# Two KV heads in one set of partitions: even partitions hold one head, odd partitions the other

## The chip, the cores and the metric

The kernel runs on one core of a Trainium2 chip. The metric is the device time of one execution in microseconds (us), the median of several runs. Engines are named as in the profile: PE is TensorE (PEld its weight loads), DVE VectorE, ACT ScalarE, POOL GpSimd, SP SyncE, whose queue issues nearly all DMAs here.

## The reference

One token of a decoder layer, batch 1, float32. The layer norm of x feeds attention over a cached window and a gated MLP, and both are added to x:

```python
xn = layernorm(x)                                    # x: 1 x 1 x 1024
q = (xn @ wq).reshape(32 heads, 128)                 # wq: 1024 x 4096
k, v = k_cache[:, :, -4096:, :], v_cache[:, :, -4096:, :]   # 4 KV heads, 8 query heads to each
p = softmax(q @ k.T * 128 ** -0.5)                   # 32 x 4096
a = (p @ v).reshape(4096) @ wo                       # wo: 4096 x 1024
h = gelu(xn @ w_gate) * (xn @ w_up)                  # 1024 x 3584 each, tanh form
out = x + a + h @ w_down                             # w_down: 3584 x 1024
```

The weights and the two windows of the cache come to 94.4 MB, each byte of which is used once. The window of one KV head is 4096 keys of 128 numbers, 2 MB.

## The kernel before

All weights and cache rows pass through one tile, `ring`, of 128 partitions with 32768 floats each. `PLAN` (L39) lists 17 loads: a key such as ("k", 0), the column of the ring where it begins, and the older load whose place it takes. `used(key)` (L121) issues the loads that wait for `key`, and the main loop (L441) goes through the plan in the same order and consumes each load. So the order of all DMAs is written by hand: wq in two loads of 8.4 MB, then k and v of heads 0 and 1, half of w_gate, k and v of heads 2 and 3, the rest of w_gate, w_up, wo, w_down. All go through SP's queue, in that order. A DMA that overwrites a piece of the ring is held on SP until the engines that read this piece are done, and what stands behind it on SP waits too.

Rows of a matrix are split between PE and DVE in `project` (L227): rows r = 0 and 2 go to PE (`blocks`), rows 1 and 3 are scaled and added into `part` by DVE (L210, L212), and `projected` adds `part` at the end.

A window of keys is read by `window` (L76): partition p takes keys 32p to 32p + 31, 16 KB in one piece. ("k", 0) is two DMAs, head 0 to columns 0 to 4095 of the ring and head 1 to columns 4096 to 8191; ("v", 0) goes to the next 8192 columns likewise, and ("k", 1), ("v", 1) take the same places for heads 2 and 3. For each head `transpose_keys` (L265) makes 32 transposes on PE (`kt_p`), which ACT copies to `kT` (L272), eight copies to a head. `scores` (L275) multiplies them by the head's queries in `qz`; `s_p` then has eight query heads' scores in four quadrants of 32 partitions, 1024 to each. DVE takes the maximum of each partition (L283) and makes `negm`, ACT the exponentials with their sum `l` (L286). `values` (L291) transposes the weights and multiplies them by v into `o_p`. A head's softmax is thus in four parts, one for each quadrant, each with its own maximum; `maxima`, `factors` and `normalizers` bring them to one maximum and one sum, later and away from the loads, and `heads` (L346) weighs `o_p` by them and adds the parts up on PE with `pick`.

Instructions of each engine run in the order in which the code issues them; nothing reorders them.

Of the kernel before, what the change touches and what calls it, by code (L numbers as in the profile page):

```python
# [9 lines left out]
F32 = mybir.dt.float32  # L10
# [5 lines left out]
P = 128  # L16
# [17 lines left out]
SCALE = DH ** -0.5  # L34
GELU_C = math.sqrt(2.0 / math.pi)
# [15 lines left out]
def tile_decode_layer(  # L51
# [24 lines left out]
    def window(cache, g):  # L76
        return cache[0, g, SK - WIN:, :].rearrange("(p j) d -> p j d", p=P)
# [27 lines left out]
    def load(key, at):  # L105

        parts = {("d", 2): 2, ("d", 3): 4}.get(key, 1)
        first = at
        for src in sources(*key):
            rows, n = src.shape[1:]  # L110
            dst = ring[:, at:at + rows * n].rearrange("p (t n) -> p t n", n=n)
            at += rows * n
            step = rows // parts
            for t in range(0, rows, step):
                cuts = 2 if key == ("d", 3) and t == rows - 1 else 1
                for cut in range(cuts):
                    cols = slice(cut * n // cuts, (cut + 1) * n // cuts)
                    nc.sync.dma_start(dst[:, t:t + step, cols], src[:, t:t + step, cols])  # L118
# [26 lines left out]
    qz = consts.tile([P, HKV, 32], F32, name="qz")  # L145
# [97 lines left out]
    def queries():  # L243
# [3 lines left out]
        for b in range(2):  # L247
            for hh in range(4):
# [5 lines left out]
                qz[:, 2 * b:2 * b + 2, 0:8].rearrange("p s (t h) -> p s t h", t=2),  # L254
# [3 lines left out]

    m = work.tile([P, HKV], F32, name="m")
    negm = work.tile([P, HKV], F32, name="negm")  # L260
    l = work.tile([P, HKV], F32, name="l")
# [13 lines left out]
    def scores(g):  # L275
        kT = keys.pop(g)
        s_p = psum.tile([P, 2, NB], F32, name="s_p", tag="s")
        for i in range(8):
            b, c = divmod(i, 4)
            nc.tensor.matmul(  # L280
                s_p[32 * c:32 * c + 32, b, :], qz[:, g, :], kT[:, i, :], start=True, stop=True
            )
        nc.vector.reduce_max(m[:, g:g + 1], s_p, axis=AX.XY)  # L283
        nc.vector.tensor_scalar(negm[:, g:g + 1], m[:, g:g + 1], -SCALE, None, op0=ALU.mult)
        p = work.tile([P, 2, NB], F32, name="p", bufs=2)
        nc.scalar.activation(  # L286
            p, s_p, AF.Exp, bias=negm[:, g:g + 1], scale=SCALE, accum_out=l[:, g:g + 1]
        )
# [26 lines left out]
    top = work.tile([HKV, 4, 32], F32, name="top")  # L315
    weight = work.tile([P, HKV], F32, name="weight")
    sel = same.rearrange("p c h -> p (c h)")

    def maxima():
        mt_p = small("mt_p")  # L320
        nc.tensor.transpose(mt_p[:HKV, :P], m, ident)
        nc.vector.reduce_max(
            top[:, 0, :], mt_p[:HKV, :P].rearrange("g (c h) -> g h c", c=4), axis=AX.X
# [4 lines left out]
    def factors():  # L328
        mm_p = small("mm_p")
        nc.tensor.transpose(mm_p[:, :HKV], top.rearrange("g c h -> g (c h)"), ident[:HKV, :HKV])  # L330
        d = work.tile([P, HKV], F32, name="d")
        nc.vector.tensor_sub(d, m, mm_p[:, :HKV])
        e = work.tile([P, HKV], F32, name="e")
# [12 lines left out]
    def heads():  # L346
        o_sb = work.tile([P, HKV, DH], F32, name="o_sb")
        for g in range(HKV):
            nc.vector.tensor_scalar(
                o_sb[:, g, :], o_p[:, g, :], weight[:, g:g + 1], None, op0=ALU.mult  # L350
# [4 lines left out]
        for odd in range(2):  # L355
            nc.tensor.matmul(
                ot_p, pick[:, odd].rearrange("p o h s -> p (o h s)"),
                o_sb.rearrange("p (a o) d -> p o a d", o=2)[:, odd],
                start=odd == 0, stop=odd == 1,
            )  # L360
# [149 lines left out]
```

## Time and profile before

| | |
|---|---|
| median of 3 runs | 229.1 us (229.05 to 229.22) |
| the profiled execution | 229.1 us; its span on the core is 227.3 us, so 1.8 us lie around it |
| read from HBM | 94.38 MB, 415 GB/s over the span |
| busy share of the span | PE 53%, DVE 43%, ACT 15%, POOL 0% |
| DMA engines | SP's queue q1 takes 97.0% of the 16 engines' span |
| granted TensorE clock | 0.797 |

Busy shares are averages over stages. The row of 40 slices says how busy each engine and the DMA engines are in time; the chain that ended last says what the end of the program hung on, followed back step by step.

### The profile page before, as it was taken

How to read it: one execution, taken by the hardware profiler on the slowest of the kernel's cores; microseconds unless marked ns; L12 is line 12 of the kernel's file. 1: busy time of each engine (PE TensorE's matmuls, PEld its weight loads, DVE VectorE, ACT ScalarE, POOL GpSimd, SP SyncE). 2: the span in 40 equal slices, each digit the busy share in tenths (PEclk: the TensorE clock that was granted, in tenths of full speed). 3: DMA queues.
4: the chain of work that ended last, by engine and by line, in shares of the span. 5: the costliest groups of instructions: out<-in, count | busy, mean ns of one | idle time of the engine just before them, and what ended most of it. 6: DMA issues, size and time to landing. Idle time of an engine off the chain costs nothing.

```text
span 227.3 us, 2496 instructions
## 1 busy us (share of the span) xinstructions
PE 120.4 (53%) x1100; PEld 62.9 (28%) x1100; DVE 97.0 (43%) x105; ACT 33.1 (15%) x57; POOL 0.7 (0%) x6
## 2 busy tenths in 40 slices
PE   0120900687866888595745390255219906452754
PEld 0010200154453746364511010111004903121322
DVE  7030920690202091201149489158219606993600
ACT  2000000054174307453200310000000000000000
POOL 1000000000000000000000000000000000000000
PEclk9999975599679699978879978559956655875879
DMA  9899899799999799999999999999999999999991
GB/s 369 370 461 462 369 484 438 334 438 421 437 484 484 327 424 417 421 510 428 394 407 434 439 469 454 394 493 392 430 461 392 438 412 415 421 456 395 424 385 51
DMA packets 3774, 94.53 MB, mean 416 GB/s; under 512 B 426, under 2 KB 434, under 8 KB 1076
## 3 DMA queue, kind: packets, MB, share of 16 engines
q1 hardware_dynamic: 3752, 94.38, 97.0%
q8 instruction: 8, 0.13, 0.2%
q14 instruction: 2, 0.02, 0.0%
q10 hardware_dynamic: 12, 0.01, 0.0%
HBM read 94.38 MB, written 0.00 MB: 415 GB/s over the span
## 4 chain that ended last, share of the span: by engine, by line
DMA 79%; DVE 14%; PE 5%; issue 0%; SPq 0%; DVEq 0%
DMA ring<-in_B_w_gate 26%; DMA ring<-in_A_wq 18%; DMA ring<-in_A_wo 14%; DVE part L212 13%; DMA ring<-in_B_w_up 11%; DMA ring<-in_B_w_down 10%; PE out_p L421 5%; DVE part L210 1%; SPq L118 0%; DVE y L485 0%; DVEq L212 0%
## 5 line engine op out<-in xcount | busy, mean ns | idle before, releaser
L212 DVE SCALAR_TENSOR_TENSOR part<-ring,xz,part 128x3584 f32<-128x3584 f32 (+1 forms) x9 | 37.2, 4129 | 22.2 <-DMA ring<-in_A_wq 12.4
L271 PE MATMUL kt_p<-ident,ring 128*128 128x128 f32 x128 | 21.5, 327 | 7.0 <-ACT kT L272 6.3
L272 ACT ACTIVATE kT<-kt_p 128x512 f32<-128x512 f32 x32 | 17.8, 595 | 43.9 <-PE kt_p L271 43.9
L222 PE MATMUL acc_q<-ring,xz 128*32 128x512 f32 x64 | 11.1, 858 | 22.2 <-DMA ring<-in_A_wq 22.2
L212 DVE SCALAR_TENSOR_TENSOR out_part<-ring,oz,out_part 128x1024 f32<-128x1024 f32 x15 | 19.3, 1285 | 7.9 <-DMA ring<-in_A_wo 7.4
L421 PE MATMUL out_p<-ring,hz 128*32 128x256 f32 x160 | 14.5, 520 | 13.7 <-DMA ring<-in_B_w_down 13.7
L421 PE MATMUL out_p<-ring,oz 128*32 128x256 f32 x128 | 12.3, 569 | 17.0 <-DMA ring<-in_A_wo 17.0
L271 PEld LDWEIGHTS kt_p<-ident,ring 128*128 128x128 f32 x128 | 16.4, 163 | 15.2 <-ACT kT L272 9.6
L222 PE MATMUL acc_u<-ring,xz 128*32 128x512 f32 x56 | 10.8, 838 | 10.7 <-DMA ring<-in_B_w_up 7.0
L283 DVE TENSOR_REDUCE m<-s_p 128x1 f32<-128x1024 f32 x4 | 4.9, 1224 | 26.7 <-PE s_p L280 26.7
L210 DVE TENSOR_SCALAR part<-ring,xz 128x3584 f32<-128x3584 f32 (+1 forms) x3 | 6.5, 2172 | 14.8 <-DMA ring<-in_A_wq 7.4
L421 PEld LDWEIGHTS out_p<-ring,hz 128*32 128x32 f32 x160 | 6.7, 146 | 21.5 <-DMA ring<-in_B_w_down 12.3
L421 PEld LDWEIGHTS out_p<-ring,oz 128*32 128x32 f32 x128 | 5.5, 162 | 23.9 <-DMA ring<-in_A_wo 18.0
L308 PE MATMUL o_p<-ring,pT 128*32 128x128 f32 x256 | 9.5, 309 | 4.7 <-ACT pT L303 4.7
L212 DVE SCALAR_TENSOR_TENSOR out_part<-ring,hz,out_part 128x1024 f32<-128x1024 f32 x8 | 10.3, 1285 | 3.9 <-DMA ring<-in_B_w_down 3.6
L222 PE MATMUL acc_g<-ring,xz 128*32 128x512 f32 x56 | 8.9, 719 | 4.5 <-DMA ring<-in_B_w_gate 4.5
L222 PEld LDWEIGHTS acc_q<-ring,xz 128*32 128x32 f32 x64 | 2.6, 150 | 29.8 <-issue 15.8
L308 PEld LDWEIGHTS o_p<-ring,pT 128*32 128x32 f32 x256 | 8.0, 123 | 5.8 <-ACT pT L303 5.8
L280 PE MATMUL s_p<-kT,qz 128*32 128x512 f32 x64 | 8.4, 645 | 0.0
L222 PEld LDWEIGHTS acc_u<-ring,xz 128*32 128x32 f32 x56 | 2.1, 138 | 17.6 <-DMA ring<-in_B_w_up 7.7
L178 PE MATMUL xt_p<-ident,x_rows 2*128 2x2 f32 x4 | 0.6, 252 | 10.4 <-DMA x_rows<-in_A_x 10.4
L300 PE MATMUL pt_p<-ident,p 128*128 128x128 f32 x32 | 5.9, 347 | 0.0
(94 smaller groups left out, 76.8 us busy)
## 6 DMA issues: line engine op xcount, KB each, us to landing
ring<-in_B_w_gate SPq DMA_DIRECT2D x2, 7168.0 KB
ring<-in_A_k_cache SPq DMA_DIRECT2D x4, 2048.0 KB
ring<-in_A_v_cache SPq DMA_DIRECT2D x4, 2048.0 KB, 23.3
ring<-in_B_w_down SPq DMA_DIRECT2D x2, 4096.0 KB, 24.3
ring<-in_B_w_up SPq DMA_DIRECT2D x2, 3584.0 KB, 26.3
ring<-in_B_w_up SPq DMA_DIRECT2D x1, 7168.0 KB
ring<-in_B_w_down SPq DMA_DIRECT2D x2, 2048.0 KB, 23.8
ring<-in_B_w_down SPq DMA_DIRECT2D x3, 512.0 KB
```

What stands on the lines that cost most here:

```text
L178: nc.tensor.transpose(xt_p[:, r * NJ:(r + 1) * NJ], x_rows[:, r:NR * P:NR], ident[:NJ, :NJ])
L210: nc.vector.tensor_scalar(total, w, factor, None, op0=ALU.mult)
L212: nc.vector.scalar_tensor_tensor(total, w, factor, total, op0=ALU.mult, op1=ALU.add)
L222: nc.tensor.matmul(acc[kind][32 * c:32 * c + 32, b, :], z, w[:, n * NB:(n + 1) * NB], start=start, stop=stop,)
L271: nc.tensor.transpose(t_p[:, jj * P:(jj + 1) * P], kn[:, j * DH:(j + 1) * DH], ident)
L272: nc.scalar.activation(kT[:, i, :], t_p, AF.Copy)
L280: nc.tensor.matmul(s_p[32 * c:32 * c + 32, b, :], qz[:, g, :], kT[:, i, :], start=True, stop=True)
L283: nc.vector.reduce_max(m[:, g:g + 1], s_p, axis=AX.XY)
L300: nc.tensor.transpose(t_p[:, jj * P:(jj + 1) * P], p[:, b, jj * P:(jj + 1) * P], ident)
L308: nc.tensor.matmul(o_p[32 * c:32 * c + 32, g, :], pT[:, b, jj, 32 * c:32 * c + 32], vn[:, j * DH:(j + 1) * DH], start=(b == 0 and jj == 0) ...
L421: nc.tensor.matmul(out_p[32 * c:32 * c + 32, :], z, w[:, c * CO:(c + 1) * CO], start=start, stop=stop)
```

## The change

`window` now splits the 4096 keys of a head over 64 partitions instead of 128, so each partition takes 64 keys, 32 KB in one piece. The first head of a pair goes to partitions 0, 2, 4, ..., the second to 1, 3, 5, ..., both over the same 8192 columns. There are still eight DMAs of 2 MB for keys and values.

One pass over half of the columns (`transpose_keys`, `scores`, `values` with index g) now has half of the keys of both heads. Its transposes put the two heads' keys in alternate columns, `qz` holds the 16 query heads of a pair, and the scores of a query against the other head's keys are made too and thrown away: `away` is 0 for the head's own keys and -1e30 for the others. It enters the maximum (taken for even and odd columns apart and then joined) and the bias of the exponential, which is made for even and odd columns in two instructions. Each head's softmax is in eight parts, four quadrants times two passes, and `maxima` to `heads` join eight.

```diff
     def window(cache, g):
-        return cache[0, g, SK - WIN:, :].rearrange("(p j) d -> p j d", p=P)
+        return cache[0, g, SK - WIN:, :].rearrange("(p j) d -> p j d", p=P // 2)
...
         first = at
+        if key[0] in "kv":
+            for odd, src in enumerate(sources(*key)):
+                dst = ring[odd:P:2, at:at + RING // 4]
+                nc.sync.dma_start(dst, src.rearrange("p j d -> p (j d)"))
+            loaded[key] = ring[:, at:at + RING // 4]
+            return
...
-    pick = consts.tile([P, 2, 2, REP, 8], F32, name="pick")
-    nc.vector.memset(pick, 0.0)
-    for odd in range(2):
-        nc.vector.tensor_copy(
-            pick[:, odd, odd], same[:, 0, 0:REP].unsqueeze(2).to_broadcast([P, REP, 8])
-        )
+    pick = consts.tile([P, 2 * REP, 8], F32, name="pick")
+    nc.vector.tensor_copy(pick, same[:, 0, 0:2 * REP].unsqueeze(2).to_broadcast([P, 2 * REP, 8]))
...
+    away = consts.tile([P, 2], F32, name="away")
+    nc.vector.reduce_sum(away[:, 1:2], same[:, 0, REP:2 * REP], axis=AX.X)
+    nc.vector.tensor_scalar(away[:, 0:1], away[:, 1:2], -FAR, None, op0=ALU.mult)
+    nc.vector.tensor_scalar(away[:, 1:2], away[:, 1:2], FAR, -FAR, op0=ALU.mult, op1=ALU.add)
...
             nc.tensor.matmul(
-                s_p[32 * c:32 * c + 32, b, :], qz[:, g, :], kT[:, i, :], start=True, stop=True
-            )
-        nc.vector.reduce_max(m[:, g:g + 1], s_p, axis=AX.XY)
-        nc.vector.tensor_scalar(negm[:, g:g + 1], m[:, g:g + 1], -SCALE, None, op0=ALU.mult)
+                s_p[32 * c:32 * c + 32, b, :], qz[:, g // 2, :], kT[:, i, :], start=True, stop=True
+            )
+        s = s_p.rearrange("p b (n odd) -> p odd (b n)", odd=2)
+        m2 = work.tile([P, 2], F32, name="m2")
+        nc.vector.reduce_max(m2, s, axis=AX.X)
+        nc.vector.tensor_add(m2, m2, away)
+        nc.vector.reduce_max(m[:, g:g + 1], m2, axis=AX.X)
+        nc.vector.scalar_tensor_tensor(
+            bias[:, g, :], m[:, g:g + 1].to_broadcast([P, 2]), -SCALE, away, op0=ALU.mult, op1=ALU.add
+        )
         p = work.tile([P, 2, NB], F32, name="p", bufs=2)
-        nc.scalar.activation(
-            p, s_p, AF.Exp, bias=negm[:, g:g + 1], scale=SCALE, accum_out=l[:, g:g + 1]
-        )
+        for odd in range(2):
+            nc.scalar.activation(
+                p.rearrange("p b (n odd) -> p odd (b n)", odd=2)[:, odd], s[:, odd], AF.Exp,
+                bias=bias[:, g, odd:odd + 1], scale=SCALE, accum_out=l[:, g, odd:odd + 1],
+            )
...
         mt_p = small("mt_p")
-        nc.tensor.transpose(mt_p[:HKV, :P], m, ident)
+        for f in range(2):
+            nc.tensor.transpose(mt_p[:2, f * P:(f + 1) * P], m[:, f:HKV:2], ident)
...
         le = work.tile([P, HKV], F32, name="le")
-        nc.vector.tensor_mul(le, l, e)
+        nc.vector.tensor_add(le, l[:, :, 0], l[:, :, 1])
+        nc.vector.tensor_mul(le, le, e.rearrange("p g f -> p (g f)"))
...
-        r = work.tile([P, HKV], F32, name="r")
-        nc.vector.reciprocal(r, ls_p[:, :HKV])
-        nc.vector.tensor_mul(weight, e, r)
+        r = work.tile([P, 2], F32, name="r")
+        nc.vector.reduce_sum(r, ls_p[:, :HKV].rearrange("p (g f) -> p g f", f=2), axis=AX.X)
+        nc.vector.reciprocal(r, r)
+        nc.vector.tensor_mul(weight, e, r.unsqueeze(2).to_broadcast([P, 2, 2]))
...
-        for g in range(HKV):
+        for g in range(2):
             nc.vector.tensor_scalar(
-                o_sb[:, g, :], o_p[:, g, :], weight[:, g:g + 1], None, op0=ALU.mult
+                o_sb[:, g, :], o_p[:, 2 * g, :], weight[:, g, 0:1], None, op0=ALU.mult
+            )
+            nc.vector.scalar_tensor_tensor(
+                o_sb[:, g, :], o_p[:, 2 * g + 1, :], weight[:, g, 1:2], o_sb[:, g, :],
+                op0=ALU.mult, op1=ALU.add,
             )
...
-        for odd in range(2):
-            nc.tensor.matmul(
-                ot_p, pick[:, odd].rearrange("p o h s -> p (o h s)"),
-                o_sb.rearrange("p (a o) d -> p o a d", o=2)[:, odd],
-                start=odd == 0, stop=odd == 1,
-            )
+        nc.tensor.matmul(ot_p, pick.rearrange("p h s -> p (h s)"), o_sb, start=True, stop=True)
```

SP's queue, from the first keys to the second half of w_gate, before the change. Each row is a DMA with its destination's partitions and floats and the semaphores that it is held for: DMAHW are landings of earlier DMAs, PE and DVE are counts of work done there.

```order
L118 DMA ring<-in_A_k_cache 128x4096 [waits DMAHW1_49,PE_49]
L118 DMA ring<-in_A_k_cache 128x4096 [waits DMAHW0_49,DVE_49]
L118 DMA ring<-in_A_v_cache 128x4096 [waits PE_49]
L118 DMA ring<-in_A_v_cache 128x4096 [waits DMAHW2_49,DVE_49]
L118 DMA ring<-in_B_w_gate 128x14336 [waits DMAHW3_49,DMAHW6_49,DVE_49,PE_49]
L118 DMA ring<-in_A_k_cache 128x4096 [waits DMAHW7_49,DMAHW4_49,PE_49]
L118 DMA ring<-in_A_k_cache 128x4096 [waits DMAHW5_49,DMAHW0_49,PE_49]
L118 DMA ring<-in_A_v_cache 128x4096 [waits DMAHW1_49,PE_49]
L118 DMA ring<-in_A_v_cache 128x4096 [waits DMAHW2_49,PE_49]
L118 DMA ring<-in_B_w_gate 128x14336 [waits DMAHW3_49,DVE_49,PE_49]
```

The same piece of SP's queue after the change:

```order
L113 DMA ring<-in_A_k_cache 64x8192 [waits DMAHW1_49,DVE_49,PE_49]
L113 DMA ring<-in_A_k_cache 64x8192 [waits DMAHW0_49]
L113 DMA ring<-in_A_v_cache 64x8192 [waits DVE_49,PE_49]
L113 DMA ring<-in_A_v_cache 64x8192 [waits DMAHW2_49]
L125 DMA ring<-in_B_w_gate 128x14336 [waits DMAHW3_49,DMAHW6_49,DVE_49,PE_49]
L113 DMA ring<-in_A_k_cache 64x8192 [waits DMAHW7_49,DMAHW4_49,PE_49]
L113 DMA ring<-in_A_k_cache 64x8192 [waits DMAHW5_49,DMAHW0_49]
L113 DMA ring<-in_A_v_cache 64x8192 [waits DMAHW1_49,PE_49]
L113 DMA ring<-in_A_v_cache 64x8192 [waits DMAHW2_49]
L125 DMA ring<-in_B_w_gate 128x14336 [waits DMAHW3_49,DVE_49,PE_49]
```

Of each pair of loads it is now the first that is held for PE, and for all the work on the whole stretch of 8192 columns; before, each was held for the work on its own 4096.

DVE's queue around the first two `scores`, before (`part` is the sum of `project`, `qz` the queries, `m` the maxima):

```order
L253 COPY qz<-q_p 128x2x8 x2
L283 TENSOR_REDUCE m<-s_p 128x1
L284 TENSOR_SCALAR negm<-m 128x1
L283 TENSOR_REDUCE m<-s_p 128x1
L284 TENSOR_SCALAR negm<-m 128x1
L210 TENSOR_SCALAR part<-ring,xz 128x3584
```

And after the change, where `m_271` and `m_337` are the tiles `m2` of two passes:

```order
L263 COPY qz<-q_p 128x16 x2
L297 TENSOR_REDUCE m_271<-s_p 128x2
L298 TENSOR_TENSOR m_271<-m_271,away 128x2
L299 TENSOR_REDUCE m<-m_271 128x1
L300 SCALAR_TENSOR_TENSOR bias<-m,away 128x2
L297 TENSOR_REDUCE m_337<-s_p 128x2
L298 TENSOR_TENSOR m_337<-m_337,away 128x2
L299 TENSOR_REDUCE m<-m_337 128x1
L300 SCALAR_TENSOR_TENSOR bias<-m,away 128x2
L220 TENSOR_SCALAR part<-ring,xz 128x3584
```

Two instructions between the scores and the exponentials have become four. The places of PE's and ACT's work in their queues are the same as before.

More of the change, by code (lines that the diff above doesn't have):

```diff
@@ L34 @@
 SCALE = DH ** -0.5
+FAR = 1e30
 GELU_C = math.sqrt(2.0 / math.pi)
@@ L144, in tile_decode_layer @@
     nc.vector.memset(xz, 0.0)
[L145 removed]
+    qz = consts.tile([P, 2, 32], F32, name="qz")
     nc.vector.memset(qz, 0.0)
@@ L259, in tile_decode_layer @@
     m = work.tile([P, HKV], F32, name="m")
-    negm = work.tile([P, HKV], F32, name="negm")
-    l = work.tile([P, HKV], F32, name="l")
+    bias = work.tile([P, HKV, 2], F32, name="bias")
+    l = work.tile([P, HKV, 2], F32, name="l")
     keys, probs = {}, {}
@@ L312, in values @@
                     )
-    top = work.tile([HKV, 4, 32], F32, name="top")
-    weight = work.tile([P, HKV], F32, name="weight")
+    top = work.tile([2, 4, 32], F32, name="top")
+    weight = work.tile([P, 2, 2], F32, name="weight")
     sel = same.rearrange("p c h -> p (c h)")
```

15 lines of the change are left out of this document (8 added, 7 removed).

## The prediction

> **What bounds the kernel now.** I read the page first: the row of DMA slices, the queues, the chain that ended last.
>
> ```profile
> span 227.3 us, 2496 instructions
> ...
> DMA  9899899799999799999999999999999999999991
> ...
> q1 hardware_dynamic: 3752, 94.38, 97.0%
> ...
> DMA 79%; DVE 14%; PE 5%; issue 0%; SPq 0%; DVEq 0%
> ```
>
> The reader is to see that the 16 DMA engines are busy in every slice but the last, 97.0% with the one queue that SP fills. The DVE and PE parts of the chain (14% and 5%) are no time in which loads stood still: the slices are full there too. So two things can change the time: the pace of the bytes, and a moment at which the queue has nothing left. Work on PE, DVE and ACT counts only through the second.
>
> For the pace I took windows in which one kind of row flows: wq (64 KB pieces), keys and values (16 KB pieces, two stretches), w_gate (56 KB pieces).
>
> ```profile
> 2.00:21.00 19.00, 1.75 (x8) 1.55 (x8) 5.49 (x27) 1.49 (x2) 0.00 (x0) 1.00 0.96 411
> 42.00:61.00 19.00, 16.94 (x117) 8.28 (x118) 10.23 (x5) 5.37 (x9) 0.00 (x0) 0.86 1.08 460
> ...
> 78.00:97.00 19.00, 15.37 (x164) 9.47 (x163) 7.41 (x4) 8.36 (x16) 0.00 (x0) 0.95 1.00 423
> 98.00:114.00 16.00, 11.70 (x173) 8.55 (x171) 2.00 (x6) 5.54 (x10) 0.00 (x0) 0.85 0.98 420
> ```
>
> The last two columns are the DMA engines' busy share and GB/s. Divided by the share (a window cuts large packets), the pace is 428 and 429 GB/s with large pieces (411/0.96, 420/0.98) and 426 and 423 with the 16 KB pieces.
>
> For the second I took SP's timeline: how early each load is issued.
>
> ```profile
> 51.02 0.33 SPq L118 DMA_DIRECT2D ring<-in_B_w_gate  x1
> 52.07 17.53 SPq L118 DMA_DIRECT2D ring<-in_A_k_cache  x2
> 77.24 4.10 SPq L118 DMA_DIRECT2D ring<-in_A_v_cache  x2
> 86.14 0.33 SPq L118 DMA_DIRECT2D ring<-in_B_w_gate  x1
> 98.76 26.12 SPq L118 DMA_DIRECT2D ring<-in_B_w_up  x3
> 140.75 18.12 SPq L118 DMA_DIRECT2D ring<-in_A_wo  x2
> ...
> 224.82 0.62 SPq L486 DMA_DIRECT2D out_y<-y  x1
> ```
>
> A row with x2 runs from the first issue to the end of the second, so the second keys of ("k", 1) were issued at 52.07 + 17.53 - 0.33 = 69.27 and the second values at 81.01. What SP waited for, and the end of the output:
>
> ```profile
> SPq L118 <- PE kt_p L271: 26.3, 3, 16.8
> ...
> SPq L118 <- PE o_p L308: 10.9, 2, 7.6
> ...
> SPq L506 <- DMA out_y<-y: 0.8, 1, 0.8
> ```
>
> The 4 KB output lands 0.8 us after its issue ends, 0.62 + 0.8 = 1.4 us after it begins. I take 1.4 us as the time by which a load has to be issued before its bytes are wanted.
>
> When the loads land is seen from who was waiting for them:
>
> ```profile
> 41.89 5.04 PE L222 MATMUL acc_q<-ring,xz 128*32 128x512 f32 x32 [13.09 <-DMA ring<-in_A_wq]
> ...
> 46.86 0.85 PEld L271 LDWEIGHTS kt_p<-ident,ring 128*128 128x128 f32 x8 [0.84 <-DMA ring<-in_A_k_cache]
> ...
> 50.89 1.15 PE L271 MATMUL kt_p<-ident,ring 128*128 128x128 f32 x8 [0.20 <-ACT kT L272]
> ...
> 59.91 1.97 PE L271 MATMUL kt_p<-ident,ring 128*128 128x128 f32 x8
> ...
> 80.00 2.09 DVE L210 TENSOR_SCALAR part<-ring,xz 128x3584 f32<-128x3584 f32 x1 [7.37 <-DMA ring<-in_B_w_gate]
> ...
> 85.00 1.06 PE L271 MATMUL kt_p<-ident,ring 128*128 128x128 f32 x8 [0.63 <-DMA ring<-in_A_k_cache]
> ...
> 112.44 0.34 DVE L326 COPY top<-top 4x32 f32<-4x32 f32 x3
> 116.55 3.95 DVE L212 SCALAR_TENSOR_TENSOR part<-ring,xz,part 128x3584 f32<-128x3584 f32 x1 [3.77 <-DMA ring<-in_B_w_gate]
> ```
>
> wq is there at 41.89 and head 0's keys at 46.86: 5.0 us for 2 MB. w_gate lands at 80.0 and head 2's keys at 85.0, so head 3's at about 90.0 and its values behind them.
>
> **The change part by part.** *The eight loads.* Bytes and number of DMAs stay. The pieces double to 32 KB. At the pace of the largest pieces, 428.5 instead of 424.5 GB/s, the 16.8 MB would take 39.2 instead of 39.5 us; going from four pieces per 64 KB to two I take two thirds of the difference: -0.2 us. That holds if 16 engines write to 64 partitions as fast as to 128. No load in this trace goes to fewer than 128 partitions but x's few rows. Bounds: -0.35 us where the pieces run as the largest do; on the other side the pace per partition is kept instead of that per engine, and 64 partitions take the bytes at half the rate, 39.5 us more. The rows don't separate the two, since engines and partitions are always all in use. The nearest is that the pace hardly depends on the piece or on the source (423 to 429 GB/s), which is a fixed width somewhere between engine and partition, and both readings fit it. I take -0.2: each DMA still has 64 pieces for 16 engines, and its partitions lie over the whole range, as now.
>
> The Trainium skill's "SBUF — State Buffer", section "Door 1: The DMA port swizzle (why `[64,N]` ≈ `[32,N]`)", speaks on both sides of this: partitions share 16 ports, groups of four neighbours to a port, so 0 to 63 reach only eight ports and half of the rate, while every other partition up to 127 reaches all sixteen. By that coverage the sum stays at -0.2. But the Trainium skill's "DMA: Bandwidth & Descriptors", section "Why a DMA increments its semaphore by 16 and not by 1", gives each of 16 engines an equal share, four pieces here; if those are four consecutive ones, engine e writes partitions 8e to 8e + 6, two ports one after the other, together with engine e + 4, and at any time eight ports stand idle: an estimate by these two pages of the Trainium skill of twice the time, +39.5 us. No run so far shows which pieces an engine gets.
>
> *The start of the keys' work.* A pass now needs both heads' loads, so the first transposes wait from 46.86 to 51.8, one load later: +4.9 us. PE then stands idle from 46.9 to 51.8. At a low clock two groups of transposes take 1.97 us (the row at 59.91), at the full one 1.15; so if the clock drops in that pause, each two of the pass's eight groups cost 0.8 us more while it is low: 0 to 3.3 us; I take one and a half such rows, 1.2 us. +6.1 us.
>
> *The softmax of a pass.* Prices:
>
> ```profile
> L272 ACT ACTIVATE kT<-kt_p 128x512 f32<-128x512 f32 x32 | 17.8, 595 | 43.9 <-PE kt_p L271 43.9
> ...
> L283 DVE TENSOR_REDUCE m<-s_p 128x1 f32<-128x1024 f32 x4 | 4.9, 1224 | 26.7 <-PE s_p L280 26.7
> ...
> L286 ACT ACTIVATE p<-s_p,negm 128x1024 f32<-128x1024 f32 x4 | 4.5, 1115 | 8.5 <-DVE negm L284 8.5
> ...
> L356 PE MATMUL ot_p<-o_sb,pick 128*128 128x256 f32 x4 | 2.1, 674 | 5.6 <-DVE o_sb L349 5.6
> ...
> L349 DVE TENSOR_SCALAR o_sb<-o_p,weight 128x128 f32<-128x128 f32 x4 | 1.1, 341 | 0.0
> ...
> L286 ACT ACTIVATION_READ_ACCUMULATOR p<-s_p,negm 128x1 f32 x4 | 0.8, 192 | 0.0
> ...
> L284 DVE TENSOR_SCALAR negm<-m 128x1 f32<-128x1 f32 x4 | 0.6, 153 | 0.1
> ...
> L184 DVE TENSOR_REDUCE st<-xt 128x1 f32<-128x8 f32 x1 | 0.2, 163 | 0.0
> ...
> L332 DVE TENSOR_TENSOR d<-m,mm_p 128x4 f32<-128x4 f32 x1 | 0.2, 151 | 0.0
> ```
>
> DVE: the large maximum stays at 1.22 if alternate columns cost nothing (bounds: the same, or twice that), then 0.15 + 0.16 + 0.15 in place of 0.15: +0.35 with the gaps. ACT: two of 0.6 and two sums of 0.19 in place of 1.12 + 0.19: +0.25. Per pass +0.6, by the second pass of a pair +1.2. The rest is small: two `mt_p` transposes for one and a sum and a reduction more in `factors` and `normalizers`, some 0.6 us in all; `heads` has the same four steps of about 0.34 and saves half of PE's 2.1 us; setup is done long before PE's first data. All this lies under loads that are already queued.
>
> *The issue of later loads.* Held now for both passes, the keys of ("k", 1) are issued not at 52.07 and 69.27 but both at 69.27 + 6.1 + 0.6 = 76.0; wanted at 80.0 - 1.4 = 78.6. The values are issued not at 77.24 and 81.01 but both at 81.01 + 6.1 + 1.2 = 88.3; wanted when the second keys end, 90.0 - 1.4 = 88.6. That is the narrowest place: 0.3 us to spare, with an uncertainty of 1.5 us from the clock. Bounds of a pause there: 0 and 2 us; I take 0.3. Behind the values on SP stands w_gate's second half: it needs PE's part of the first half, then at 86.14 + 7.3 = 93.4, wanted at about 98. Further on PE is 7.3 + 1.2 = 8.5 us late, so DVE's copies of `top` end at 112.78 + 8.5 = 121.3 and its `part` starts there instead of at 116.55, 4.7 us late. w_up's last load goes out at 98.76 + 26.12 - 0.33 + 4.7 = 129.3, two to three us before the loads ahead of it (17 us behind 116.55) are through, and wo at 145.5 instead of 140.75. These are hidden, and the next landing of w_up brings all engines back in step.
>
> Sum against the profiled execution, which took 229.1, the median itself: 229.1 - 0.2 + 0.3 = 229.2 us.
>
> **The rivals.** *A: the loads keep their pace and SP is in time (the forecast).* For it: 64 pieces for 16 engines, slack at all places but one. 228.7 to 229.6.
>
> *B: engines crowd, and the time ends on the other side, slower.* In every row each engine holds a share of all 128 partitions; with 64, engines may stand in each other's way at the same few. For it: the pace of 423 to 429 GB/s looks like a width that can't be shared by two. Against it: the range of partitions is as wide as before. Each per cent lost on 39.5 us costs 0.4 us, so a loss above 1.5% decides; at half the pace it is 229.1 + 39.5 = 268.6; engines that fall out of step lose less, so 240 to 268, with 262 as its middle. The two pages of the Trainium skill named above come to the same, if an engine's pieces are consecutive. Work on PE is then no issue: loads are later than it.
>
> *C: the values are issued late.* With clock windows that fall badly, 0.5 to 3 us without loads at about 90: 229.7 to 232.
>
> *D: larger pieces bring more,* up to the -0.35 of the bound and something at the engines that end last: 228.3 to 228.6. The doubling may also not take place if a piece of 32 KB is moved as two; that is within A.
>
> **How the numbers follow.** A 0.38, C 0.12, D 0.05, B 0.45. A, C and D are one case as to the loads' pace, 0.55 together, and A is its middle, so the time is 229.2. A measurement of this kernel tells about 0.2% (0.46 us) from no change: faster 0.05 (D), same 0.38 (A), slower 0.57 (B and C). The likeliest case's own range is 228.6 to 230.5; to leave out no more than 2 in 10 the range has to take in most of B: 228.6 to 266.
>
> **What would show it.** In the profile after: the share and GB/s in 42 to 61 and 78 to 97 (423 to 430 per full share means A; less, or keys that land more than 5 us after one another, B); the DMA slices at 88 to 91 (a gap means C); SP's issues of keys and values in pairs near 76 and 88; PE's first transposes near 51.8; DVE's large maximum at 1.22 us or more. The prediction is wrong if the time between PE's first transposes and wq's landing is near 20 us instead of 10.

## The result, and the profile after

The median of five executions is 234.5 us (233.56 to 234.83) against 229.08 us (229.04 to 229.22) of the kernel before on the same chip: a ratio of 1.0226, interval 1.0211 to 1.024. The change makes the kernel 5.4 us slower. The profiled execution took 234.09 us. Here and below medians are over all executions, while ratios leave out those more than 1.5% above a kernel's fastest, one of them 245.43 us long at a granted clock of 0.58 (the last kernel of the eighth experiment).

The page of the kernel after, the lines that answer to the first fence of the prediction:

```profile
span 232.3 us, 2509 instructions
...
DMA  9898998999999597899989999899999999999991
...
q1 hardware_dynamic: 3240, 94.38, 95.5%
...
DMA 55%; PE 24%; DVE 13%; ACT 5%; issue 1%; SPq 0%; ACTq 0%; DVEq 0%
```

The row of DMA slices now has a 5 (the slice from 75.5 us) and a 7 (from 87.1 us). The kernel before also has two 7s without a pause, so a 7 by itself proves nothing. Nor does DMA's part of the chain that ended last, which fell from 79% to 55%: it is 54% in the first experiment, which loses no time. Windows of the same kernel show the pace and the two holes; the columns end with PE's granted clock, the DMA engines' busy share and GB/s:

```profile
42.00:61.00 19.00, 15.13 (x80) 7.35 (x80) 8.97 (x2) 5.14 (x9) 0.00 (x0) 0.67 1.06 455
77.20:79.00 1.80, 1.80 (x16) 0.76 (x18) 0.00 (x0) 1.06 (x2) 0.00 (x0) 0.70 0.00 0
79.20:82.00 2.80, 1.76 (x16) 0.86 (x8) 1.83 (x5) 0.04 (x1) 0.00 (x0) 1.00 1.07 339
89.60:91.60 2.00, 2.00 (x41) 0.92 (x36) 0.00 (x0) 0.00 (x0) 0.00 (x0) 1.00 0.06 16
...
42.00:105.00 63.00, 48.10 (x388) 28.09 (x388) 20.36 (x18) 22.76 (x43) 0.00 (x0) 0.79 0.97 404
```

While loads flow, 64 partitions take them as fast as 128 did: 455/1.06 = 429 GB/s, before 460/1.08 = 426. But in the 1.8 us after 77.2 no packet of a load begins, and in the 2.0 us after 89.6 hardly any. A window counts a packet, with all of its bytes, where it begins, so packets that began earlier still run there; by the packet records of the trace (beginning, duration and size of every packet) the 16 engines stand idle for 1.64 us on average at the first hole and 1.80 at the second. Behind a hole the engines are all busy and yet move only 339 GB/s. Over the whole stretch the kernel before has:

```profile
42.00:105.00 63.00, 50.24 (x436) 30.00 (x436) 20.80 (x14) 27.15 (x47) 0.00 (x0) 0.87 1.01 432
```

(432 - 404) x 63 / 432 = 4.1 us of loads are missing by 105 us, but the packets at the two edges make this uncertain. With the bytes of each packet spread over its time, the packet records put the changed kernel behind the kernel before by 2.4 us at 84 us, 5.0 at 96 us and 4.9 at 200 us. So all of the 5.0 us between the two profiled executions arise at the two holes, and nothing is lost later. The holes lie where a load was issued too late. SP's timeline of the kernel after:

```profile
77.91 1.11 SPq L113 DMA_DIRECT2D ring<-in_A_k_cache  x2
90.50 1.11 SPq L113 DMA_DIRECT2D ring<-in_A_v_cache  x2
94.39 0.33 SPq L125 DMA_DIRECT2D ring<-in_B_w_gate  x1
...
150.02 13.88 SPq L125 DMA_DIRECT2D ring<-in_A_wo  x2
```

Keys of ("k", 1) go out after the queue has run dry, and so do the values. In the packet records the first packet begins 1.26 us after the beginning of each of these two issues (79.17 and 91.76). Why SP came so late is in PE's timeline of the kernel after:

```profile
51.77 6.92 PE L283 MATMUL kt_p<-ident,ring 128*128 128x128 f32 x32 [3.37 <-DMA ring<-in_A_k_cache]
58.62 1.92 PE L232 MATMUL acc_q<-part,unit 128*32 128x512 f32 x16
...
63.99 3.08 PE L292 MATMUL s_p<-kT,qz 128*32 128x512 f32 x16
67.00 1.58 PE L283 MATMUL kt_p<-ident,ring 128*128 128x128 f32 x8
72.31 5.57 PE L283 MATMUL kt_p<-ident,ring 128*128 128x128 f32 x24 [3.73 <-ACT kT L284]
77.81 2.13 PE L292 MATMUL s_p<-kT,qz 128*32 128x512 f32 x16
79.87 1.09 PE L320 MATMUL pt_p<-ident,p 128*128 128x128 f32 x8
84.00 2.64 PE L328 MATMUL o_p<-ring,pT 128*32 128x128 f32 x64 [3.04 <-ACT pT L323]
```

The kernel before, at the same steps:

```profile
51.97 1.92 PE L222 MATMUL acc_q<-part,unit 128*32 128x512 f32 x16
...
57.34 2.63 PE L280 MATMUL s_p<-kT,qz 128*32 128x512 f32 x16
59.91 1.97 PE L271 MATMUL kt_p<-ident,ring 128*128 128x128 f32 x8
64.56 4.68 PE L271 MATMUL kt_p<-ident,ring 128*128 128x128 f32 x24 [2.68 <-ACT kT L272]
69.17 1.92 PE L280 MATMUL s_p<-kT,qz 128*32 128x512 f32 x16
71.03 1.09 PE L300 MATMUL pt_p<-ident,p 128*128 128x128 f32 x8
74.47 2.73 PE L308 MATMUL o_p<-ring,pT 128*32 128x128 f32 x64 [2.35 <-ACT pT L303]
```

The first pass is done at 58.62 instead of 51.97 (+6.65): both heads' keys have to be there, and then all 32 transposes take 6.92 us, most of them at half the clock. The window below has PE's granted clock in the third column from the end:

```profile
50.98:57.80 6.82, 6.03 (x27) 5.06 (x28) 0.12 (x1) 3.40 (x6) 0.00 (x0) 0.50 0.97 418
```

The second pass is done with its transposes at 77.81 instead of 69.17 (+8.64). The 2.0 us more have three parts. The first scores take 3.01 us to the next transposes (63.99 to 67.00) instead of 2.57. From there to the transposes that wait for ACT's copies of `kT` it is 5.31 us (67.00 to 72.31) instead of 4.65, because ACT makes the exponentials first, as before, and these now come later and are two. The remaining transposes take 5.50 us instead of 4.61, at a granted clock of 0.50 from 71.45 to 78.28. Before the values, from `pt_p` to `o_p`, it is 4.13 us instead of 3.44. So the softmax costs 0.66 and 0.69 us in the two passes. In the groups by line it is as priced:

```profile
L305 ACT ACTIVATE p<-s_p,bias 128x512 f32<-128x512 f32 x8 | 5.6, 710 | 9.9 <-DVE bias L300 9.9
L297 DVE TENSOR_REDUCE m<-s_p 128x2 f32<-128x1024 f32 x4 | 4.9, 1224 | 36.6 <-PE s_p L292 36.6
```

The maximum over alternate columns costs the same 1224 ns as before; an exponential of half the columns 710 ns where 600 was assumed.

### The profile page after: what moved, and what is told of

The parts are those of the page before. It is cut to its first block, busy times and chain, and to the rows that moved or that the text cites. A ratio compares the mean times of both kernels' runs of the same rounds, so it can differ in the third digit from the quotient of the medians.

```text
span 232.3 us, 2509 instructions
## 1 busy us (share of the span) xinstructions
PE 127.1 (55%) x1099; PEld 64.9 (28%) x1099; DVE 98.5 (42%) x116; ACT 34.7 (15%) x65; POOL 0.7 (0%) x6
## 4 chain that ended last, share of the span: by engine, by line
DMA 55%; PE 24%; DVE 13%; ACT 5%; issue 1%; SPq 0%; ACTq 0%; DVEq 0%
DMA ring<-in_A_wo 13%; DMA ring<-in_B_w_down 11%; DMA ring<-in_A_k_cache 11%; DMA ring<-in_B_w_up 10%; DMA ring<-in_A_wq 9%; PE kt_p L283 9%; DVE part L222 7%; PE o_p L328 4%; PE s_p L292 4%; DVE out_part L222 3%; PE acc_q L232 2%; DVE m L297 2%; ACT p L305 2%; PE acc_g L232 2%; ACT kT L284 1%
## 5 line engine op out<-in xcount | busy, mean ns | idle before, releaser
L283 PE MATMUL kt_p<-ident,ring 128*128 128x128 f32 x128 | 24.5, 363 | 10.9 <-ACT kT L284 7.4
L284 ACT ACTIVATE kT<-kt_p 128x512 f32<-128x512 f32 x32 | 18.4, 597 | 50.9 <-PE kt_p L283 50.9
L283 PEld LDWEIGHTS kt_p<-ident,ring 128*128 128x128 f32 x128 | 19.3, 185 | 19.3 <-ACT kT L284 10.7
L232 PE MATMUL acc_q<-ring,xz 128*32 128x512 f32 x64 | 12.1, 924 | 22.7 <-DMA ring<-in_A_wq 22.7
L445 PE MATMUL out_p<-ring,hz 128*32 128x256 f32 x160 | 15.2, 516 | 14.0 <-DMA ring<-in_B_w_down 14.0
L297 DVE TENSOR_REDUCE m<-s_p 128x2 f32<-128x1024 f32 x4 | 4.9, 1224 | 36.6 <-PE s_p L292 36.6
L292 PE MATMUL s_p<-kT,qz 128*32 128x512 f32 x64 | 9.1, 688 | 0.0
L232 PE MATMUL acc_g<-ring,xz 128*32 128x512 f32 x56 | 7.7, 596 | 0.0
L305 ACT ACTIVATE p<-s_p,bias 128x512 f32<-128x512 f32 x8 | 5.6, 710 | 9.9 <-DVE bias L300 9.9
L232 PE MATMUL acc_g<-part,unit 128*32 128x512 f32 x14 | 3.6, 1061 | 5.0 <-DVE part L222 5.0
```

The source lines that it names most:

```text
L232: nc.tensor.matmul(acc[kind][32 * c:32 * c + 32, b, :], z, w[:, n * NB:(n + 1) * NB], start=start, stop=stop,)
L283: nc.tensor.transpose(t_p[:, jj * P:(jj + 1) * P], kn[:, j * DH:(j + 1) * DH], ident)
L284: nc.scalar.activation(kT[:, i, :], t_p, AF.Copy)
L292: nc.tensor.matmul(s_p[32 * c:32 * c + 32, b, :], qz[:, g // 2, :], kT[:, i, :], start=True, stop=True)
L297: nc.vector.reduce_max(m2, s, axis=AX.X)
L305: nc.scalar.activation(p.rearrange("p b (n odd) -> p odd (b n)", odd=2)[:, odd], s[:, odd], AF.Exp, bias=bias[:, g, odd:odd + 1], scale=SC ...
```

## The experiments

The theory after the result: the loads keep their pace, and the whole loss comes from keys and values that SP issues too late, because every load of a pair is now held for both passes. Rivals: writes to 64 partitions are slower in some way; the longer softmax; the low clock. All ratios are to the kernel before, run on the same chip (229.1 to 229.2 us).

**1. Half-partition loads without the longer wait.** Each load is cut by columns, so that a DMA brings one pass's columns of one head; partitions stay alternate.

```diff
-            for odd, src in enumerate(sources(*key)):
-                dst = ring[odd:P:2, at:at + RING // 4]
-                nc.sync.dma_start(dst, src.rearrange("p j d -> p (j d)"))
+            cuts = 2 if True else 1
+            n = RING // 4 // cuts
+            for cut in range(cuts):
+                for odd, src in enumerate(sources(*key)):
+                    dst = ring[odd:P:2, at + cut * n:at + (cut + 1) * n]
+                    nc.sync.dma_start(
+                        dst, src.rearrange("p j d -> p (j d)")[:, cut * n:(cut + 1) * n]
+                    )
```

> The changed kernel with each of its key and value loads cut into two by columns, first halves of both heads ahead: still every other partition, but 16 KB pieces, and a pass waits for, and holds, only its own columns, as in the kernel before. Theory (loads issued late leave the queue empty twice, the pattern of partitions costs nothing): no gap at 77 and 89 us, 229.0 to 229.6 us. Rival 1 (loads to 64 alternate partitions are slower in themselves): stays at 233 to 235 us. Rival 2 (the longer softmax made the loads late): 231 to 233 us, with gaps left.

Measured 229.01 us, ratio 1.0002 (0.9992 to 1.0012). Its page and SP's timeline:

```profile
DMA  9899899799999799999999999899999999999991
...
52.67 18.73 SPq L116 DMA_DIRECT2D ring<-in_A_k_cache  x4
79.55 4.62 SPq L116 DMA_DIRECT2D ring<-in_A_v_cache  x4
```

No hole, and the first of four issues of keys at 52.67 instead of 77.91. So alternate partitions, the masked softmax and its eight parts cost nothing that can be measured once loads are held for one pass only.

**2. Consecutive partitions.** The rival of the prediction by itself: one head to partitions 0 to 63, the other to 64 to 127 (time only; the scores are masked as for alternate ones).

```diff
-                dst = ring[odd:P:2, at:at + RING // 4]
+                dst = ring[64 * odd:64 * odd + 64, at:at + RING // 4]
```

> The changed kernel with the first head in partitions 0 to 63 and the second in 64 to 127, instead of every other; masks and picks are left as they are, so only the time counts. If a load to 64 partitions crowds the engines when these lie together (case B of the prediction, in the place where it is likeliest), each key and value load takes up to twice as long, 2 MB in about 9.7 us instead of 4.85: 255 to 275 us. If the number of partitions doesn't matter wherever they lie, 234 to 235 us, as the changed kernel.

Measured 272.18 us, ratio 1.1875 (1.186 to 1.189). The window that gave 455 GB/s with alternate partitions:

```profile
42.00:61.00 19.00, 5.98 (x32) 1.31 (x32) 8.97 (x2) 0.00 (x0) 0.00 (x0) 0.59 0.97 200
```

The engines are as busy and move 200/0.97 = 206 GB/s, half. The crowding that the prediction gave 0.45 is real, +43 us, for 64 neighbours; for every second partition it doesn't exist.

**3. The two halves of the change apart.** The new softmax on the old loads, and the new loads with the old softmax (both for the time only: the softmax takes the keys as the other kind of load would place them). The first against the changed kernel; the second is the same lines the other way round, added to the kernel before:

```diff
-        return cache[0, g, SK - WIN:, :].rearrange("(p j) d -> p j d", p=P // 2)
+        return cache[0, g, SK - WIN:, :].rearrange("(p j) d -> p j d", p=P)
...
-        if key[0] in "kv":
-            for odd, src in enumerate(sources(*key)):
-                dst = ring[odd:P:2, at:at + RING // 4]
-                nc.sync.dma_start(dst, src.rearrange("p j d -> p (j d)"))
-            loaded[key] = ring[:, at:at + RING // 4]
-            return
```

> The changed computation on keys and values that are loaded as before (128 partitions, one head to each half of the columns); the scores then mix keys and masks that don't belong together, so only the time counts. Theory: the longer softmax moves the loads by about 1.5 us, which their slack covers: 229.0 to 229.4 us. Rival 1: the same. Rival 2 (softmax makes the loads late): 231 us or more, with gaps at 77 and 89 us.

> The computation of the kernel before on the new loads (even and odd partitions, 32 KB); a head's keys are then mixed with the other's, so only the time counts. Theory: the waits are those of the changed kernel, the passes 0.6 to 0.8 us shorter, so the keys are issued near 77 and the values near 89 us; each gap shrinks by that much, 232 to 234 us. Rival 1 (pattern): 233 to 235 us. Rival 2: back to 229.0 to 229.5 us.

The softmax alone: 228.94 us, ratio 0.999 (0.9981 to 0.9999). The loads alone: 231.74 us, ratio 1.0129 (1.0103 to 1.0154), about 2.6 to 3.0 us more than before and a little below the 232 to 234 expected. So the longer softmax costs nothing while SP has slack. Added to the longer wait it makes 2 to 3 us more (234.5 against 231.74, 1.0226 against 1.0129). These are not its instructions alone. In the profile with the old softmax the issues and the first scores are:

```profile
75.51 1.11 SPq L112 DMA_DIRECT2D ring<-in_A_k_cache  x2
86.05 1.11 SPq L112 DMA_DIRECT2D ring<-in_A_v_cache  x2
```

```profile
63.37 1.92 PE L286 MATMUL s_p<-kT,qz 128*32 128x512 f32 x16
```

The values go out 4.45 us before those of the changed kernel. The softmax makes 1.3 us of this; most of the rest is PE's clock, full here from 55.05 to 68.70 and again from 75.53 on, while in the changed kernel it was 0.50 from 64.63 to 68.04 (scores of 3.08 us) and again from 85.11 to 88.52. Whether the longer softmax brings these low stretches about or they fall so by chance is not shown.

**4. The longer wait alone.** The kernel before, with one DMA of 4 MB for the two heads in place of two of 2 MB: 128 partitions, 16 KB pieces, old softmax. What changes is what a load is held for, and that the first transposes wait for both heads' keys.

```diff
+        if key[0] in "kv":
+            cache = k_cache if key[0] == "k" else v_cache
+            src = cache[0, 2 * key[1]:2 * key[1] + 2, SK - WIN:, :]
+            dst = ring[:, at:at + RING // 4].rearrange("p (g n) -> p g n", g=2)
+            nc.sync.dma_start(dst, src.rearrange("g (p j) d -> p g (j d)", p=P))
+            loaded[key] = ring[:, at:at + RING // 4]
+            return
```

> The kernel before, with the keys of two heads in one DMA of 4 MB instead of two, and their values too: 128 partitions, 16 KB pieces and the old softmax, but PE's first transposes wait for both heads and the next pair is held for both. It does nothing else of the change. Theory (the waits are the cause): keys issued near 75 and values near 86 us, 230.5 to 233 us, as the old softmax on the new loads. Rival (alternate partitions or 32 KB pieces cost something after all): 229.0 to 229.5 us.

Measured 231.86 us, ratio 1.0113 (1.0097 to 1.0128), as expected (230.5 to 233), and the same as the new loads with the old softmax within their intervals. The pattern of partitions and the size of the pieces therefore have no part in this that can be measured; the wait does it. Its issues:

```profile
75.64 0.37 SPq L113 DMA_DIRECT2D ring<-in_A_k_cache  x1
86.18 0.37 SPq L113 DMA_DIRECT2D ring<-in_A_v_cache  x1
```

**5. PE kept warm.** Eight matmuls into a bank that is not yet in use, ahead of the first transposes, to keep the clock up while PE waits for the second head's keys.

```diff
             kn = loaded.pop(key)
+            if i == 0:
+                for _ in range(8):
+                    nc.tensor.matmul(out_p[:, 0:P], ident, ident, start=True, stop=True)
```

> The changed kernel with eight matmuls of the identity on PE (into out_p, overwritten later) between wq and the first transposes, so that PE is not idle while it waits for the second head's keys. Theory: part of the lateness is PE's low clock after that pause; the first pass gets 1 to 2 us shorter, the next keys are issued near 76 and the next values near 89 us, both gaps shrink by 1 to 2 us: 231 to 233.5 us. Rival (the clock plays no part, the pause alone and the softmax do): 234 to 235 us.

Measured 233.39 us, ratio 1.0167 (1.0148 to 1.0187), by the ratios 1.3 us below the changed kernel. Two of its six executions took 235.79 and 236.38 us, longer than any of the changed kernel, and have no trace; so the gain rests on the profile more than on the times. In the profile, where the execution took 232.87 us, the first pass is back at full clock and keys and values go out 1.4 and 1.3 us earlier. SP's timeline, and the first transposes in PE's:

```profile
76.53 1.11 SPq L113 DMA_DIRECT2D ring<-in_A_k_cache  x2
89.22 1.12 SPq L113 DMA_DIRECT2D ring<-in_A_v_cache  x2
```

```profile
51.76 1.09 PE L283 MATMUL kt_p<-ident,ring 128*128 128x128 f32 x8 [1.16 <-DMA ring<-in_A_k_cache]
```

**6. Only the order of compute moved.** All 32 KB loads stay. The queries are projected before the first transposes, and a pass's softmax follows the transposes of the next, so that ACT copies `kT` before it makes exponentials.

```diff
+        return s_p
+
+    def softmax(g, s_p):
         s = s_p.rearrange("p b (n odd) -> p odd (b n)", odd=2)
...
+            if i == 0:
+                projected("q", 8)
             transpose_keys(2 * i, kn[:, :half])
             if i == 0:
-                projected("q", 8)
                 queries()
-            scores(2 * i)
+            s_p = scores(2 * i)
             transpose_keys(2 * i + 1, kn[:, half:])
-            scores(2 * i + 1)
+            softmax(2 * i, s_p)
+            softmax(2 * i + 1, scores(2 * i + 1))
```

> The changed kernel with all eight 32 KB loads kept and only PE's and ACT's order moved: the queries of pass 0 are projected before the first transposes, and the softmax of a pass is computed after the transposes of the next one, so that ACT copies kT before it makes exponentials. Theory (the pauses come from late issues; a restart of an empty queue costs about 2 us): the second keys go out near 74 instead of 77.9, the second values near 87 instead of 90.5, the pause at 77 to 79 goes and the one at 90 shrinks; 230 to 232 us. Rival 1 (the loads themselves are slower, however early they are issued): both pauses stay in another form and the time stays at 234 to 235. Rival 2 (the order of compute is no matter, since the second half of a pair of loads sets the issue): keys still near 77, 233.5 to 235.

Measured 233.28 us, ratio 1.0157 (1.0125 to 1.0189): better than the changed kernel, but short of the 230 to 232 expected. The profiled execution is the longest of its six, 234.86 us at a mean granted clock of 0.780; the shortest took 231.18 at 0.807, and time and clock go together in the others too. SP's timeline of it:

```profile
74.89 1.11 SPq L113 DMA_DIRECT2D ring<-in_A_k_cache  x2
91.26 1.11 SPq L113 DMA_DIRECT2D ring<-in_A_v_cache  x2
```

The window around the values' issue, with the DMA share and GB/s at its end, and the second pass's scores in PE's timeline:

```profile
86.00:92.00 6.00, 5.69 (x146) 4.88 (x149) 3.81 (x1) 1.48 (x3) 0.00 (x0) 1.00 0.26 108
```

```profile
78.31 3.64 PE L292 MATMUL s_p<-kT,qz 128*32 128x512 f32 x16 [3.45 <-ACT p L308]
```

The keys go out 3.0 us earlier, as meant. But there is one tile `s_p`, so the second pass's scores now wait 3.45 us for the exponentials of the first, and the values go out 0.8 us later than in the changed kernel. The instructive part is that the hole at 77 is gone (0.03 us of idle engines in the packet records of 74 to 84, 1.64 in the changed kernel) and yet this execution is no shorter: it is 0.77 us longer, and its values went out 0.76 us later. The bytes that flow earlier at 77 are missing at 90, where the engines now stand idle for 4.6 us.

That gives one relation for all three profiles with a large hole at 90: the time minus the issue of the second values is 234.09 - 90.50 = 143.59 in the changed kernel, 232.87 - 89.22 = 143.65 with the warm PE and 234.86 - 91.26 = 143.60 here. Everything behind the values follows at a fixed distance, at least where the queue was empty for long. With the time of undisturbed loads, 229.0, the values have to be out by 229.0 - 143.6 = 85.4. The hole at 77 is no second cost: without it, the hole at 90 is longer by as much.

**7. Parts of the loads cut by columns.** First only ("k", 0), then ("k", 0) and ("v", 1), by the lines of the first experiment with `cuts = 2 if key == ("k", 0) else 1`, and with `key in (("k", 0), ("v", 1))`.

> The changed kernel with only the first keys (heads 0 and 1) cut by columns; all other key and value loads keep 32 KB pieces. Theory: PE starts about 4.9 us earlier and at the full clock, so the next keys are issued near 71 us and the next values near 84 us, both before they are wanted: 228.7 to 229.3 us, up to 0.3 below the kernel before. Rival 1 (pattern): 233 to 235 us. Rival 2 (softmax): 231 us or more, since the passes themselves stay as long.

> The changed kernel with the first keys and the second values cut by columns, the other key and value loads in 32 KB pieces. Theory: the keys of the second pair are issued near 73 us as in the kernel that cut only the first keys, the first half of the values near 81 instead of 86 us, so nothing is issued late: 228.8 to 229.3 us. Rival (something else costs time in 32 KB loads): 230 us or more.

Both miss their expectation. ("k", 0) alone: 230.66 us, ratio 1.0068 (1.0049 to 1.0086). In its shortest execution, 229.71 us, which is the profiled one, SP issued:

```profile
73.50 1.11 SPq L116 DMA_DIRECT2D ring<-in_A_k_cache  x2
85.97 1.11 SPq L116 DMA_DIRECT2D ring<-in_A_v_cache  x2
```

By the relation 85.97 gives 229.6, close to the 229.71 of that execution; the issue was expected near 84, the time at 228.7 to 229.3. ("k", 0) and ("v", 1): 230.78 us, ratio 1.006 (1.0038 to 1.0083), with executions anywhere from 229.01 to 231.66, though its profile (229.37 us) has no hole; 228.8 to 229.3 was expected. The same kernel once more:

> The same kernel as e7 once more, one look, to see an execution with a pause. Theory: if the time is above 230, the DMA slices show a gap near 76 to 79 or near 88 to 92 behind an issue of SP that is later than in the first look (keys after 73.8 or values after 82.5); if it is near 229 there is none. Rival: a time above 230 with full slices and the same issue times.

This took 229.16 us, again without a hole, so no trace of a long execution exists and the spread is not explained.

**8. The same with the softmax later,** by the lines of the sixth experiment (without those on `projected`).

> The first keys cut by columns (each DMA brings half of the columns of both heads, 16 KB pieces), the other six loads in 32 KB pieces, and the softmax of a pass after the transposes of the next. Without the second of these it was 230.7. Theory: issues of the second keys and values come 2 to 3 us earlier than in that kernel (73.5 and 86.0), and nothing is left of the pause at 87: 228.8 to 229.6. Rival (something beside the issue times costs): 230.3 to 231.

> First keys and second values cut by columns, the other four loads in 32 KB pieces, and the softmax of a pass after the transposes of the next. Without the last of these it was 230.8, with runs from 229.0 to 231.7. Theory (the spread comes from executions in which an issue is just too late): with 2 to 3 us more of slack all executions are at the loads' own pace, 228.8 to 229.4, spread below 0.6. Rival (the spread has another cause): 229 to 231.7 again.

("k", 0): 229.63 us, ratio 1.0024 (1.0006 to 1.0041), 1.0 us below the kernel without the later softmax and just outside the 228.8 to 229.6 expected. ("k", 0) and ("v", 1): 229.19 us, ratio 1.0008 (0.9995 to 1.002), the same as before. In the profile of the first, an execution of 228.96 us, the values go out at:

```profile
80.16 1.11 SPq L116 DMA_DIRECT2D ring<-in_A_v_cache  x2
```

five us ahead of 85.4, and there is no hole. Its other executions still reach 230.93, one of the second kernel 230.63, so the spread below 0.6 that was expected of the latter is not met. What differs in these executions no trace shows. One hint is on record: the executions of the first kernel up to 229.0 us had a mean granted clock of 0.790 to 0.805, those above 230 us 0.776 to 0.789, while the kernel before takes 228.97 to 229.40 us at any clock from 0.767 to 0.820. That would fit issues that come late when PE's low stretches fall badly, but a long execution may also have the lower mean for another reason; it was not tried. No version beats the kernel before by more than 0.1%: the shortest medians are 228.94 and 229.01.

## Why the prediction was wrong

It forecast 229.2 and came out at 234.5. The range held it only because it reached to the crowding of case B, which did not happen, and "slower" had 0.57 mostly for the same wrong reason; that both came true is luck. What happened is case C, given 0.12 and 229.7 to 232: the right mechanism and the right place, sized at less than half, so that 234.5 lies beyond its range and short of B's.

- **The pace, -0.2 us, and "alternate partitions are as good as all":** right as to the pace (429 GB/s against 426; 1.0002 in the first experiment). The gain is of the right size too: in the packet records the loads of the eighth experiment's first kernel, six of eight in 32 KB pieces, are 0.3 us ahead of the kernel before at 100 us. The 0.45 for case B was too much. The half rate exists for consecutive partitions (+43 us measured, +39.5 worked out for the full doubling). This agrees with the Trainium skill's "SBUF — State Buffer", section "Door 1: The DMA port swizzle (why `[64,N]` ≈ `[32,N]`)", on both sides: 64 neighbours reach half of the ports, every second partition reaches all. What failed is the estimate that combined it with an engine's four pieces being neighbours; how the pieces are dealt to the engines was not tried.
- **Two loads issued together, held for both passes:** right (x2 rows of 1.11 us). PE's first transposes at 51.77 were forecast for 51.8, and the maximum stayed at 1224 ns.
- **The start, +6.1 us:** +6.65. The wait was right (+4.9), the clock's 1.2 was 1.74 (6.85 us from the first transposes to the next step instead of 5.11). The clock was low from 50.98 to 57.80, for nearly all four rows of eight transposes and not for one and a half; on the other hand such a row then takes 1.80 us instead of 1.34, so it costs 0.46 and not 0.8, which was read from a single row.
- **The softmax, +0.6 us a pass:** right, 0.66 and 0.69. What was left out is the low clock behind the start: the first scores cost 0.44 us more and the remaining transposes 0.89. With the 0.55 of the start these make the keys go out at 77.91 instead of the 76.0 forecast. The values, forecast for 88.3, went out at 90.50, 2.2 us later. The warm PE accounts for 1.3 us of these.
- **The deadline, "wanted at 88.6, 0.3 us to spare":** this is the step that failed most. The relation above puts it at 85.4, 3.2 us earlier. Two things were wrong in it. First, 90.0 was worked out from rows of DVE and PE, that is, from when a consumer saw a landing, which is that of the last of 16 engines; on average the engines had run dry before that. In the sixth experiment the share of 0.26 in 86 to 92 is 1.6 us of work that begins there, and the packets of 1.21 us under way at 86.0 had some 0.6 us left, so the engines were dry at about 88.1, the first of them at 87.4 and the last at 89.9. That execution was 0.3 us behind by then, so the undisturbed queue is dry at about 87.8. Second, 1.4 us from issue to need came from a 4 KB write, not from a queue that starts anew: 87.8 - 85.4 = 2.4 us. So the slack was not +0.3 but -5.1 (3.2 from the deadline, 2.2 from the issue).
- **"Bounds of a pause there: 0 and 2 us":** -5.1 us of slack is all of the 5.0 us between the two profiled executions.
- **The keys, wanted by 78.6:** too late by the same error. An issue at 74.89 or 75.64 left no hole at 77, and 76.53 a partial one (0.37 us); but this cost nothing of its own.
- **w_up at 129.3 and wo at 145.5 hidden:** hidden, since the packet records have no pause between 100 and 200 us; wo went out at 150.02, 4.5 us later than forecast, with the whole program behind 90 shifted.

What stays open: the kernels with the old softmax and late loads are 1.2 us (230.94 profiled against 86.18 + 143.6 = 229.8) and 1.5 us (231.15 against 229.65) above the relation. Up to 220 us their bytes keep to it: the packet records put them 0.5 to 0.65 us behind the kernel before from 92 us on. The excess shows at the end: with one load for two heads, the DMA engines are still 0.48 busy in the window

```profile
221.00:225.00 4.00, 2.85 (x44) 0.90 (x36) 0.00 (x0) 0.00 (x0) 0.00 (x0) 1.00 0.48 184
```

where the kernel before has

```profile
221.00:225.00 4.00, 3.31 (x44) 1.46 (x36) 0.42 (x1) 0.00 (x0) 0.00 (x0) 0.84 0.33 123
```

The last 20 packets of the loads end within 1.1 us of one another there (223.68 to 224.81), in the kernel before within 0.4 us (222.84 to 223.19). So some engines end behind the others. It looks as if a small hole leaves them behind to the end, but that was not tried.

## What to carry to other kernels

In a kernel that streams through one DMA queue, the price of holding a load for more work is not read from how busy the engines are but from one subtraction: when the load is issued against when the queue runs dry. Take the second from the DMA engines themselves, allow for the start of an empty queue, and follow only the last late issue: holes ahead of it move, they don't add up. If two tensors must share a wait, cut their loads so that each DMA carries what one pass consumes; here this gave back all 5.4 us. And spread a load over few partitions by stride, not as a block.

## What the runs showed of the hardware

- A load to 64 partitions runs at full pace if they are every second one (429 GB/s per full share) and at half if they are consecutive (206 GB/s).
- An empty queue does not start at full pace: the first packet begins 1.26 us after the beginning of the issue (which itself takes 0.47), and in the packet records the first 32 KB pieces take 1.6 to 2.6 us where later ones take 1.21; the window behind the hole shows 339 GB/s with all engines busy. Together an issue has to be some 2.4 us ahead, estimated from the sixth experiment. The Trainium skill's "DMA: Bandwidth & Descriptors", section "Specifications", gives about 0.6 us to the first byte for this kind of queue; the measured time is twice that, counted from the beginning of the issue, and 0.79 us counted from its end; the measurement decides.
- PE's granted clock fell to 0.50 at 50.98, 2.6 us into a gap between matmuls (48.40 to 51.77), and stayed there until 57.80; with matmuls in that gap it was 1.00 from 48.00 to 61.66, and the first eight transposes took 1.09 us. The Trainium skill's "TensorE: Matmul & The Clock Gate", section "HAM oscillation — how this bites in real kernels", puts the limit for an idle gap at about 3.4 us. The trace bears out that the gap did it, but not the limit: the clock fell earlier, and in the kernel before it also fell, at 58.42, where no gap of the 3.4 us ahead was over 0.3 us. The measurement decides. How long the low clock lasts was not foreseen.
- In the records of the changed kernel and of the kernel before, the granted clock after 28 us is always 0.50 or 1.00, and each stretch lasts 3.41 us or a multiple of it. So a shift of a few tenths of a us can decide in which stretch a piece of PE's work falls.
